# Six query products on GpSimd, b folded into ScalarE's scales in two groups, and a new order of all steps

## The chip, the core and the metric

The kernel runs on one core of a Trainium2 chip. The core has five engines with a queue each: TensorE (PE in the profile, its weight loads PEld), VectorE (DVE), ScalarE (ACT), GpSimd (POOL) and SyncE (SP), which here only issues DMA transfers. Within its queue an engine works strictly in order; between engines semaphores order the work. The metric is the device time of one execution in microseconds (us). Before the change it is 264.83 us, the median of three runs (264.46, 264.83 and 264.94).

## The reference: what is computed

An attention with sketched polynomial features, for 4 batches, 4 heads, 1088 positions and head size 32, whose output goes straight into a feed-forward layer with a rational activation:

```python
def phi(x):                                   # 8 x 8 = 64 features of one position
    a, b = S1 @ x, S2 @ x                     # 8 numbers each
    return outer(a, b)
kv = sum over positions of phi(k) v^T;  z = sum over positions of phi(k)
attn = (phi(q) kv) / (phi(q) z + 1e-6)
h = attn @ w_in                               # 4352 tokens x 2048
P = a0 + a1*h + a2*h**2 + a3*h**3
Q = 1.0 + abs(b0)*abs(h) + abs(b1)*h**2
out = (P / (Q + 1e-6)) @ w_out                # 4352 x 128
```

## The kernel before

**Queries.** The 1024 main positions of each of the four batches are taken in chunks of 512 (four blocks of 128). The very first chunk is cut into two halves, so there are nine chunks n = 0 to 8; a tenth, n = 9, holds the 64 remaining positions of all batches. Step names count them 0, 0b, 1, 2, ... 8, so chunk n = 3 is step number 2. For each chunk `add_queries` (L584) transposes q on PE, evacuates it on ACT, projects it to a, b and a denominator part on PE, and evacuates this as `abc` on ACT. From the second batch on two chunks make a pair: DVE computes the denominators of both, inverts them and scales a by them (`den_product` to `scale`, L627 to L641). Then `product` (L643) forms the 64 features per head as `q_p`, 128 partitions x 1024 float32, by one multiplication with broadcast operands. PE transposes `q_p` (`p_transposes`, "qp tr"), ACT evacuates it (`p_evac`, "qp ev"), PE multiplies it by kv ("x mm"), and ACT evacuates `xT` ("x ev"). There is one buffer of `q_p`, so a second product waits for the first one's transposes.

**Feed-forward.** `add_group` (L779) handles 23 groups of hidden columns, g = 0 to 22; most have 128 x 4096 values. PE computes h, ACT evacuates it as bfloat16 `hb` in pieces of 1024 ("hev"). The quotient is formed as P * exp(-ln Q), with Ln and Exp on ACT. `TERMS` (L158) picks one of four forms per group:

- "2" (groups 0 to 3 and 20 to 22) and "2d" (groups 6, 8, 10, 12, 15, 17, 19): DVE does absolute value, Q and P by multiplications; in "2d" the constant a1 is added by a DMA transfer that accumulates into y ("dadd1").
- "t" (groups 5, 7, 11, 13, 16, 18): DVE makes u = |h| with a bitwise operation ("abs", L820), the square `sq` ("sq", L914) and the square scaled by b1/b0 ("sqb", L919). A DMA transfer accumulates this onto u ("dq"), and Ln takes b0 as its scale.
- "s" (groups 4, 9, 14): ACT makes u = |b0 h| with one activation (`s_abs`, L807, "habs"), DVE scales the square by b1 (L919), the transfer accumulates, and Ln's scale is 1.

In "s" and "t" P comes from `sq` too: y = a3*sq + a1 ("n1"), sq becomes a2*sq + a0 ("n3"), y is multiplied by h ("n2"), and a second transfer adds `sq` to y ("dy"). In all forms y is finally multiplied by u ("n5") and goes to PE ("py").

**The order.** Every step is registered by `plan.add(engine, ns, function, after=..., take=..., give=...)`. The list `ORDER` (L19) names the 783 steps in the order in which they are issued; each engine's queue is that list restricted to its own steps. The durations in `plan.add` are bookings with which such a list can be planned; at run time they do nothing. The accumulating transfers are issued by POOL (`accumulate`, L895), in its queue's order. `HOT` (L162) gives numbers of matmuls on zeros that stand at places of PE's queue (L1071).

**The start.** SP loads the inputs in a fixed order; POOL prepares constants, copies v into place ("va 0", "va 1", L428) and copies the small weights (`s_weights`, L374).

Of the kernel before, what the change touches and what calls it, by code (L numbers as in the profile page):

```python
# [123 lines left out]
def kernel(  # L124
# [13 lines left out]
    nc = tc.nc  # L138
# [19 lines left out]
    TERMS = {**{g:"2d" for g in range(4,20)}, **{g:"s" for g in (4,9,14)}, **{g:"t" for g in (5,7,11,13,16,18)}}  # L158
# [3 lines left out]
    HOT = [2, 6, 23, 4, 18, 4, 3]  # L162
# [26 lines left out]
    def tile_of(pool, name, shape, dtype):  # L189
        return pool.tile(shape, dtype, name=name, bufs=BUFS[name])  # L190
# [124 lines left out]
    b_rel = consts.tile([128, 3], FP, name="b_rel")  # L315
# [74 lines left out]
    def rel_b():  # L390
        nc.vector.tensor_scalar(out=b_rel[:, 0:1], in0=b_abs[:, 0:1], scalar1=1e-18, scalar2=None, op0=AX.max)
        nc.vector.reciprocal(out=b_rel[:, 1:2], in_=b_rel[:, 0:1])
        nc.vector.tensor_mul(out=b_rel[:, 2:3], in0=b_rel[:, 1:2], in1=b_abs[:, 1:2])

    c_b = plan.add("DVE", 100, abs_b, after=[ld["ab"]], rank=-5)
    c_b = plan.add("DVE", 300, rel_b, after=[c_b], rank=-5) if "t" in USED else c_b
# [187 lines left out]
    def add_queries(n, nt, srcs, weights, kv_lhs, load_steps, kv_steps, w_steps, rank, give=(), early=False,  # L584
# [58 lines left out]
        def product():  # L643
            abc = T["abc", n][:, :G, :]
            T["q_p", n] = tile_of(att, "q_p", [128, JC * H, R * R], FP)
            nc.vector.tensor_mul(out=T["q_p", n][:, :G, :].rearrange("p g (i j) -> p g i j", i=R),
                                 in0=abc[:, :, 0:R, None].broadcast_to([128, G, R, R]),
                                 in1=abc[:, :, None, R:2 * R].broadcast_to([128, G, R, R]))
# [69 lines left out]
        def rest(s):  # L718
            s = plan.add("DVE", 68 + 1067 * G // 16, product, after=[s, T.get(("prod", n - 1)) if pair == 1 else None], rank=rank + 0.02, take=["q_p"],
# [59 lines left out]
    def add_group(g, G):  # L779
# [27 lines left out]
        def s_abs():  # L807
            T["u", g] = tile_of(moe, "u", [128, GW], BF)
            nc.scalar.activation(out=T["u", g][:, :gw], in_=T["hb", g][:, :gw], func=ACT.Abs, scale=b_abs[:, 0:1])  # L809
# [18 lines left out]
        def mul(out, in0, in1):  # L828
            return lambda: nc.vector.tensor_mul(out=out(), in0=in0(), in1=in1())  # L829

        def ln(l0, lw):
            T["L", g, l0] = tile_of(moe, "L", [128, LW], FP)
            nc.scalar.activation(out=T["L", g, l0][:, :lw], in_=T["u", g][:, l0:l0 + lw], func=ACT.Ln, bias=one_ap,  # L833
                                 scale=b_rel[:, 0:1] if terms == "t" else 1.0)
# [81 lines left out]
        def s_scaled():  # L916
            T["even", g] = tile_of(moe, "lin", [128, GW], BF)
            by = b_rel[:, 2:3] if terms == "t" else b_abs[:, 1:2]
            nc.vector.tensor_scalar(out=even(), in0=sq(), scalar1=by, scalar2=None, op0=AX.mult)  # L919

        def s_affine(out, c1, c0):
            def f():
                if out is y:
                    T["y", g] = tile_of(moe, "y", [128, GW], BF)
                nc.vector.tensor_scalar(out=out(), in0=sq(), scalar1=a_sb[:, c1:c1 + 1], scalar2=a_sb[:, c0:c0 + 1],  # L925
                                        op0=AX.mult, op1=AX.add)
            return f

        if square:
            sp = plan.add("DVE", tt, s_first, after=[he], rank=g - 0.5, take=["lin"], name=f"sq {g}")  # L930
            d2 = plan.add("DVE", ts + 61, s_scaled, after=[sp, c_b], rank=g - 0.5, take=["lin"], name=f"sqb {g}")
            d = add_tile("dq", u, even, [ha, d2], g - 0.5, give=["lin"])
# [17 lines left out]
        if square:  # L950
            p = plan.add("DVE", ts + 121, s_affine(y, 3, 1), after=[sp, ld["ab"]], rank=g - 0.3, take=["y"], name=f"n1 {g}")
            t = plan.add("DVE", ts + 121, s_affine(sq, 2, 0), after=[sp, d2, p, ld["ab"]], rank=g - 0.3, name=f"n3 {g}")
            p = plan.add("DVE", tt, mul(y, y, hb), after=[p, ha], rank=g - 0.3, give=["hb"], name=f"n2 {g}")
            p = add_tile("dy", y, sq, [p, t], g - 0.3, give=["lin"])
# [158 lines left out]
```

## Time and profile before

| | |
|---|---|
| median of three runs | 264.83 us |
| the profiled execution, its own time | 264.85 us |
| its span from first to last instruction | 263.1 us |
| DVE's query products of 1024 elements | 7, mean 1.22 us |
| ACT's absolute values (L809) | 3, mean 3.74 us |
| DVE's bitwise absolute values of 4096 | 12, mean 1.25 us |
| POOL's issues of accumulating transfers (L897) | 25, 1.17 to 1.98 us each |
| these transfers, issue to landing (median) | 8.4 us |

In the profile a row of a group reads: line, engine, operation, output <- inputs, shapes, count | busy us and mean ns of one | idle time of the engine before them and what ended it. A row in order of time reads: start, duration, engine, line, operation; idle time before it in brackets. Busy time of an engine counts instructions that wait inside themselves for a resource as busy. PE's ends are modelled, so a busy PE is not a PE at its peak.

### The profile page before, as it was taken

The page shows a single profiled execution, that of the slowest core. Times are in us where ns is not written, and L with a number is a line of the kernel's source. Part 1 is how long each engine was busy: PE and PEld are TensorE (multiplying, and loading weights), DVE is VectorE, ACT ScalarE, POOL GpSimd, SP SyncE. Part 2 cuts the span into 40 slices and gives each one's busy share as a digit, 9 for nine tenths or more (in the row PEclk, how much of TensorE's full clock was granted, in tenths as well). Part 3 has the DMA queues.
Part 4 walks back from the last instruction along what each step waited for, and adds up shares of the span by engine and source line. Part 5 has one row for each costly group of instructions (what it writes and reads, how often), then busy time and mean ns, then how long its engine had stood idle before and what let it go on. Part 6 is the DMA issues. An engine that isn't in the chain of part 4 may idle for free. (4 is left out here: it accounts for less than half of the span.)

```text
span 263.1 us, 3159 instructions
## 1 busy us (share of the span) xinstructions
PE 246.8 (94%) x1186; PEld 145.6 (55%) x1186; DVE 242.8 (92%) x240; ACT 238.6 (91%) x211; POOL 43.0 (16%) x63
## 2 busy tenths in 40 slices
PE   8999999999999999989899998999999899999971
PEld 4889898755656654434373645545434345554451
DVE  1658999979999999999999999999999999999992
ACT  3249798889989999999999999999999999999993
POOL 3700010101201113011201121101220202122000
PEclk9999999999999999999999999999999999999998
DMA  6969839952888996938798879972799896788812
GB/s 171 298 209 174 166 90 173 218 91 50 189 159 96 165 190 93 118 55 150 144 133 139 156 102 181 184 139 50 133 167 128 159 187 84 91 159 162 120 40 101
DMA packets 36607, 36.94 MB, mean 140 GB/s; under 512 B 18160, under 2 KB 30448, under 8 KB 36464
## 3 DMA queue, kind: packets, MB, share of 16 engines
q0 software_dynamic: 11664, 25.69, 62.6%
q1 hardware_dynamic: 24496, 10.95, 15.8%
q8 instruction: 9, 0.15, 0.2%
q10 hardware_dynamic: 432, 0.10, 0.2%
q14 instruction: 6, 0.05, 0.1%
HBM read 8.82 MB, written 2.23 MB: 42 GB/s over the span
## 5 line engine op out<-in xcount | busy, mean ns | idle before, releaser
L794 PE MATMUL h_ps<-xT,w_in_sb 128*128 128x512 f32 (+1 forms) x320 | 126.6, 533 | 0.9 <-ACT hb L800 0.9
L794 PEld LDWEIGHTS h_ps<-xT,w_in_sb 128*128 128x128 f32 x320 | 57.4, 190 | 43.4 <-issue 34.3
L800 ACT CAST hb<-h_ps 128x1024 bf16<-128x1024 f32 (+1 forms) x70 | 70.9, 1038 | 5.6 <-PE h_ps L794 5.4
L837 ACT ACTIVATE u<-L 128x4096 bf16<-128x4096 f32 (+3 forms) x23 | 63.7, 2768 | 0.3
L829 DVE TENSOR_TENSOR y<-y,hb 128x4096 bf16<-128x4096 bf16 (+3 forms) x37 | 58.7, 1595 | 0.1
L833 ACT ACTIVATE L<-u,one_ap 128x4096 f32<-128x4096 bf16 (+3 forms) x17 | 43.4, 2555 | 0.2 <-DVE u L829 0.2
L829 DVE TENSOR_TENSOR y<-y,u 128x4096 bf16<-128x4096 bf16 (+3 forms) x23 | 39.8, 1731 | 0.5 <-ACT u L837 0.3
L857 PEld LDWEIGHTS <-w_out 128*128 128x128 bf16 x208 | 20.2, 98 | 27.6 <-issue 11.8
L857 PE MATMUL out_ps<-y,w_out 128*128 128x512 bf16 (+1 forms) x144 | 30.8, 355 | 1.1 <-DVE y L829 1.1
L897 POOL DMA_DIRECT2D u<-lin x9 | 10.8, 1206 | 104.4 <-ACT ab L461 25.7
L833 ACT ACTIVATE L<-u,one_ap,b_rel 128x4096 f32<-128x4096 bf16 x6 | 23.2, 3875 | 0.0
L914 DVE TENSOR_TENSOR lin<-hb 128x4096 bf16<-128x4096 bf16 x9 | 20.6, 2287 | 0.0
L897 POOL DMA_DIRECT2D y<-lin x9 | 12.0, 1334 | 49.6 <-DVE y L829 15.7
L829 DVE TENSOR_TENSOR u<-lin,u 128x4096 bf16<-128x4096 bf16 (+3 forms) x14 | 19.2, 1375 | 0.2
L897 POOL DMA_DIRECT2D y<-zeros x7 | 12.3, 1760 | 41.6 <-PE h_ps L794 18.4
L820 DVE TENSOR_SCALAR u<-hb 128x4096 int16<-128x4096 int16 (+3 forms) x20 | 18.4, 918 | 0.5 <-ACT hb L800 0.3
L489 PEld LDWEIGHTS kv_ps<-v_aug,k_p 128*128 128x128 f32 x128 | 15.3, 192 | 1.1 <-issue 0.2
L489 PE MATMUL kv_ps<-v_aug,k_p 128*128 128x66 f32 x128 | 15.8, 272 | 0.0
L857 PE MATMUL out_ps<-u,w_out 128*128 128x512 bf16 (+1 forms) x64 | 13.7, 352 | 1.3 <-ACT u L837 1.1
L1075 PE MATMUL kv_ps<-const-float32-0.0 128*128 128x512 bf16 x60 | 14.2, 381 | 0.0
L661 ACT COPY q_pT<-w_ps 128x512 f32<-128x512 f32 (+1 forms) x20 | 10.5, 552 | 2.6 <-PE w_ps L654 2.6
L841 DVE TENSOR_SCALAR y<-hb,a_sb 128x4096 bf16<-128x4096 bf16 (+3 forms) x14 | 12.4, 886 | 0.0
(102 smaller groups left out, 274.1 us busy)
## 6 DMA issues: line engine op xcount, KB each, us to landing
u<-lin POOLq DMA_DIRECT2D x9, 1024.0 KB, 7.9
y<-lin POOLq DMA_DIRECT2D x9, 1024.0 KB, 8.2
y<-zeros POOLq DMA_DIRECT2D x6, 1024.0 KB, 11.0
out_dram<-oT SPq DMA_DIRECT2D x7, 256.0 KB, 2.7
kq<-in_k_dram SPq DMA_DIRECT2D x3, 512.0 KB, 5.0
v_aug<-in_v_dram SPq DMA_DIRECT2D x12, 128.0 KB, 4.7
kq<-in_q_dram SPq DMA_DIRECT2D x3, 512.0 KB, 4.8
w_in_sb<-in_moe_w_in_dram SPq DMA_DIRECT2D x1, 1024.0 KB, 6.9
```

The source lines that it names most:

```text
L489: nc.tensor.matmul(T["kv", b][:, hp * 66:(hp + 1) * 66], lhsT=lhs(hp), rhs=rhs(hp), start=(first and hp == 0), stop=final, skip_group_chec ...
L794: nc.tensor.matmul(T["h", g, s][:, i * W:(i + 1) * W], lhsT=w_in_sb[:, fi * 128:(fi + 1) * 128], rhs=T["xT", n][:, :W], start=True, stop=True)
L800: nc.scalar.copy(out=T["hb", g][:, s * W:(s + nsub) * W], in_=T["h", g, s][:, :nsub * W])
L820: nc.vector.tensor_scalar(out=u().bitcast(mybir.dt.int16), in0=hb().bitcast(mybir.dt.int16), scalar1=0x7FFF, scalar2=None, op0=AX.bitwise_and)
L829: return lambda: nc.vector.tensor_mul(out=out(), in0=in0(), in1=in1())
L833: nc.scalar.activation(out=T["L", g, l0][:, :lw], in_=T["u", g][:, l0:l0 + lw], func=ACT.Ln, bias=one_ap, scale=b_rel[:, 0:1] if terms == ...
L837: nc.scalar.activation(out=T["u", g][:, l0:l0 + lw], in_=T["L", g, l0][:, :lw], func=ACT.Exp, scale=-1.0)
L841: nc.vector.tensor_scalar(out=y(), in0=hb(), scalar1=a_sb[:, 3:4], scalar2=a_sb[:, 2:3], op0=AX.mult, op1=AX.add)
L857: nc.tensor.matmul(T["o", n][:, :W], lhsT=W_terms[w][:, fis[i], :], rhs=T[src, g][:, i * W:(i + 1) * W], start=(start and i == 0), stop=(s ...
L897: nc.gpsimd.dma_start(out=dst(), in_=src(), accum_op=AX.add, max_dma_last_dim=4096)
L914: nc.vector.tensor_mul(out=sq(), in0=hb(), in1=hb())
L1075: nc.tensor.matmul(hot_ps[0], lhsT=zero.broadcast_to([128, 128]), rhs=zero.broadcast_to([128, CW]), start=True, stop=True)
```

## The change

Six query products, those of chunks n = 3 to 8 (steps 2 to 7), are made by GpSimd instead of VectorE. Group 9 goes from form "s" to form "t". In the two groups left in form "s" (4 and 14), ScalarE now makes u = |h b0/b1|, the square is accumulated without being scaled, and Ln takes b1 as its scale; P's even part goes to a second tile, since the transfer now reads `sq` itself. `ORDER` and `HOT` are new.

```diff
-    TERMS = {**{g:"2d" for g in range(4,20)}, **{g:"s" for g in (4,9,14)}, **{g:"t" for g in (5,7,11,13,16,18)}}
+    TERMS = {**{g:"2d" for g in range(4,20)}, **{g:"s" for g in (4,14)}, **{g:"t" for g in (5,7,9,11,13,16,18)}}
...
-    HOT = [2, 6, 23, 4, 18, 4, 3]
+    QPOOL = {3,4,5,6,7,8}
+    HOT = [2, 2, 5, 11, 6, 14, 14, 4, 3]
...
-        nc.vector.tensor_scalar(out=b_rel[:, 0:1], in0=b_abs[:, 0:1], scalar1=1e-18, scalar2=None, op0=AX.max)
-        nc.vector.reciprocal(out=b_rel[:, 1:2], in_=b_rel[:, 0:1])
-        nc.vector.tensor_mul(out=b_rel[:, 2:3], in0=b_rel[:, 1:2], in1=b_abs[:, 1:2])
+        nc.vector.tensor_scalar(out=b_rel[:, 0:2], in0=b_abs[:, 0:2], scalar1=1e-18, scalar2=None, op0=AX.max)
+        nc.vector.reciprocal(out=b_rel[:, 2:4], in_=b_rel[:, 0:2])
+        nc.vector.tensor_mul(out=b_rel[:, 4:5], in0=b_rel[:, 2:3], in1=b_abs[:, 1:2])
+        nc.vector.tensor_mul(out=b_rel[:, 5:6], in0=b_rel[:, 3:4], in1=b_abs[:, 0:1])
...
-            nc.vector.tensor_mul(out=T["q_p", n][:, :G, :].rearrange("p g (i j) -> p g i j", i=R),
+            eng = nc.gpsimd if n in QPOOL else nc.vector
+            eng.tensor_mul(out=T["q_p", n][:, :G, :].rearrange("p g (i j) -> p g i j", i=R),
...
-            s = plan.add("DVE", 68 + 1067 * G // 16, product, after=[s, T.get(("prod", n - 1)) if pair == 1 else None], rank=rank + 0.02, take=["q_p"],
+            s = plan.add("POOL" if n in QPOOL else "DVE", 2300 * G // 16 if n in QPOOL else 68 + 1067 * G // 16, product, after=[s, T.get(("prod", n - 1)) if pair == 1 else None], rank=rank + 0.02, take=["q_p"],
...
-            nc.scalar.activation(out=T["u", g][:, :gw], in_=T["hb", g][:, :gw], func=ACT.Abs, scale=b_abs[:, 0:1])
+            nc.scalar.activation(out=T["u", g][:, :gw], in_=T["hb", g][:, :gw], func=ACT.Abs, scale=b_rel[:, 5:6])
...
-                                 scale=b_rel[:, 0:1] if terms == "t" else 1.0)
+                                 scale={"t": b_rel[:, 0:1], "s": b_rel[:, 1:2]}.get(terms, 1.0))
...
-            d2 = plan.add("DVE", ts + 61, s_scaled, after=[sp, c_b], rank=g - 0.5, take=["lin"], name=f"sqb {g}")
-            d = add_tile("dq", u, even, [ha, d2], g - 0.5, give=["lin"])
+            if wide_abs:
+                d1 = plan.add("DVE", ts + 121, s_affine(y, 3, 1), after=[sp, ld["ab"]], rank=g - 0.45, take=["y"], name=f"n1 {g}")
+                t = plan.add("DVE", ts + 121, s_affine(even, 2, 0), after=[sp, d1, ld["ab"]], rank=g - 0.45, take=["lin"], name=f"n3 {g}")
+                d = add_tile("dq", u, sq, [ha, t], g - 0.5, give=["lin"])
+            else:
+                d2 = plan.add("DVE", ts + 61, s_scaled, after=[sp, c_b], rank=g - 0.5, take=["lin"], name=f"sqb {g}")
+                d = add_tile("dq", u, even, [ha, d2], g - 0.5, give=["lin"])
```

The new order on POOL, from the first accumulating transfer on (q prod is a query product, the others are issues of transfers):

```
before: dq 4, dy 4, dq 5, dy 5, dadd1 6, dq 7, dy 7, dadd1 8, dq 9, dy 9, dadd1 10, dq 11, dy 11, dadd1 12, dq 13, dy 13, dq 14, dy 14, dadd1 15, ...
after:  dq 4, dy 4, q prod 2, dq 5, q prod 3, dy 5, dadd1 6, dq 7, dy 7, dadd1 8, q prod 4, dq 9, q prod 5, dy 9, dadd1 10, dq 11, dy 11, dadd1 12,
        dq 13, dy 13, q prod 6, q prod 7, dq 14, dy 14, dadd1 15, ...
```

On DVE, ACT and PE the steps change places nearly everywhere after the first 15; within a group their order is mostly kept. At the start POOL makes the weight copies of the first batch between "va 0" and "va 1" instead of after both. On SP only the stores of chunks 1 and 2 change places.

More of the change, by code (lines that the diff above doesn't have):

```diff
@@ L314 @@
     b_abs = consts.tile([128, 2], FP, name="b_abs")
-    b_rel = consts.tile([128, 3], FP, name="b_rel")
+    b_rel = consts.tile([128, 6], FP, name="b_rel")
     c_add = {i: zeros if i == ADDED[0] else big.tile([128, CW], FP, name=f"c_add{i}") for i in ADDED}
@@ L390, in rel_b @@
     def rel_b():
-        nc.vector.tensor_scalar(out=b_rel[:, 0:1], in0=b_abs[:, 0:1], scalar1=1e-18, scalar2=None, op0=AX.max)
-        nc.vector.reciprocal(out=b_rel[:, 1:2], in_=b_rel[:, 0:1])
-        nc.vector.tensor_mul(out=b_rel[:, 2:3], in0=b_rel[:, 1:2], in1=b_abs[:, 1:2])
+        nc.vector.tensor_scalar(out=b_rel[:, 0:2], in0=b_abs[:, 0:2], scalar1=1e-18, scalar2=None, op0=AX.max)
+        nc.vector.reciprocal(out=b_rel[:, 2:4], in_=b_rel[:, 0:2])
+        nc.vector.tensor_mul(out=b_rel[:, 4:5], in0=b_rel[:, 2:3], in1=b_abs[:, 1:2])
+        nc.vector.tensor_mul(out=b_rel[:, 5:6], in0=b_rel[:, 3:4], in1=b_abs[:, 0:1])
     c_b = plan.add("DVE", 100, abs_b, after=[ld["ab"]], rank=-5)
-    c_b = plan.add("DVE", 300, rel_b, after=[c_b], rank=-5) if "t" in USED else c_b
+    c_b = plan.add("DVE", 400, rel_b, after=[c_b], rank=-5) if USED & {"s", "t"} else c_b
     def scaled(i, col, half):
@@ L645, in product @@
             T["q_p", n] = tile_of(att, "q_p", [128, JC * H, R * R], FP)
-            nc.vector.tensor_mul(out=T["q_p", n][:, :G, :].rearrange("p g (i j) -> p g i j", i=R),
-                                 in0=abc[:, :, 0:R, None].broadcast_to([128, G, R, R]),
-                                 in1=abc[:, :, None, R:2 * R].broadcast_to([128, G, R, R]))
+            eng = nc.gpsimd if n in QPOOL else nc.vector
+            eng.tensor_mul(out=T["q_p", n][:, :G, :].rearrange("p g (i j) -> p g i j", i=R),
+                           in0=abc[:, :, 0:R, None].broadcast_to([128, G, R, R]),
+                           in1=abc[:, :, None, R:2 * R].broadcast_to([128, G, R, R]))
         def p_transposes(hp):
@@ L917, in s_scaled @@
             T["even", g] = tile_of(moe, "lin", [128, GW], BF)
-            by = b_rel[:, 2:3] if terms == "t" else b_abs[:, 1:2]
-            nc.vector.tensor_scalar(out=even(), in0=sq(), scalar1=by, scalar2=None, op0=AX.mult)
+            nc.vector.tensor_scalar(out=even(), in0=sq(), scalar1=b_rel[:, 4:5], scalar2=None, op0=AX.mult)
         def s_affine(out, c1, c0):
             def f():
-                if out is y:
-                    T["y", g] = tile_of(moe, "y", [128, GW], BF)
+                if out is not sq:
+                    name = "y" if out is y else "lin"
+                    T["y" if out is y else "even", g] = tile_of(moe, name, [128, GW], BF)
                 nc.vector.tensor_scalar(out=out(), in0=sq(), scalar1=a_sb[:, c1:c1 + 1], scalar2=a_sb[:, c0:c0 + 1],
@@ L950, in add_group @@
         if square:
[L951 to L954, printed above, removed]
+            if not wide_abs:
+                d1 = plan.add("DVE", ts + 121, s_affine(y, 3, 1), after=[sp, ld["ab"]], rank=g - 0.3, take=["y"], name=f"n1 {g}")
+                t = plan.add("DVE", ts + 121, s_affine(sq, 2, 0), after=[sp, d2, d1, ld["ab"]], rank=g - 0.3, name=f"n3 {g}")
+            p = plan.add("DVE", tt, mul(y, y, hb), after=[d1, ha], rank=g - 0.3, give=["hb"], name=f"n2 {g}")
+            p = add_tile("dy", y, even if wide_abs else sq, [p, t], g - 0.3, give=["lin"])
         else:
```

70 rows, old and new, of the table ORDER are left out of this document.

## The prediction

> **What bounds the kernel now.** I read the page's busy shares first, then busy time by stretch, then the groups of VectorE, ScalarE and GpSimd by shape, and last the order of time around the few places where GpSimd and VectorE work at once.
>
> ```profile
> PE 246.8 (94%) x1186; PEld 145.6 (55%) x1186; DVE 242.8 (92%) x240; ACT 238.6 (91%) x211; POOL 43.0 (16%) x63
> ```
>
> Three engines stand above 90%, so the average names no bound. Busy time by stretch does (columns: PE, PEld, DVE, ACT, POOL busy us with instruction counts, clock, DMA share, GB/s):
>
> ```profile
> 0.00:22.00 22.00, 20.14 (x130) 16.27 (x131) 9.69 (x24) 9.15 (x21) 7.83 (x38) 1.00 0.80 220
> 22.00:57.00 35.00, 35.00 (x210) 28.17 (x209) 33.25 (x59) 29.93 (x37) 2.51 (x2) 1.00 0.83 160
> 57.00:250.00 193.00, 185.62 (x777) 96.81 (x776) 191.84 (x143) 191.12 (x143) 32.66 (x23) 1.00 0.82 132
> 250.00:263.20 13.20, 6.09 (x73) 4.34 (x71) 8.00 (x18) 8.40 (x13) 0.00 (x0) 0.92 0.19 70
> ```
>
> From 57 to 250 us DVE is busy 191.8 of 193.0 us and ACT 191.1: both are full at once. DVE is also nearly full from 22 to 57 us (33.3 of 35.0), ACT is not (29.9). So every microsecond that DVE gains or loses after 22 us moves the end, a gain only until ACT's own work becomes the longer. PE has 14.2 us of matmuls on zeros in its busy time and is no bound. POOL has room in its queue; the question is whether its work lies beside DVE's.
>
> The prices, from the groups by shape (columns: busy us, mean ns of one, idle before):
>
> ```profile
> L646 DVE TENSOR_TENSOR q_p<-abc 128x1024 f32<-128x1024 f32 x7 | 8.5, 1221 | 0.1
> L919 DVE TENSOR_SCALAR lin<-lin,b_abs 128x4096 bf16<-128x4096 bf16 x3 | 3.9, 1285 | 0.1
> L820 DVE TENSOR_SCALAR u<-hb 128x4096 int16<-128x4096 int16 x12 | 15.0, 1247 | 0.1
> L809 ACT ACTIVATE u<-hb,b_abs 128x4096 bf16<-128x4096 bf16 x3 | 11.2, 3736 | 0.0
> L833 ACT ACTIVATE L<-u,one_ap 128x4096 f32<-128x4096 bf16 x9 | 34.1, 3793 | 0.0
> L833 ACT ACTIVATE L<-u,one_ap,b_rel 128x4096 f32<-128x4096 bf16 x6 | 23.2, 3875 | 0.0
> ```
>
> And the two engines side by side, in order of time (start, us, engine, instruction):
>
> ```profile
> 6.49 0.62 POOL L428 COPY v_aug<-q_p 128x512 f32<-128x512 f32 x1 [1.41 <-DMA q_p<-in_v_dram]
> ...
> 7.44 1.22 DVE L472 TENSOR_TENSOR k_p<-ab 128x1024 f32<-128x1024 f32 x1 [1.48 <-ACT ab L461]
> ...
> 8.25 0.89 POOL L428 COPY v_aug<-q_p 128x512 f32<-128x512 f32 x1 [1.14 <-DMA q_p<-in_v_dram]
> ...
> 8.58 1.63 DVE L472 TENSOR_TENSOR k_p<-ab 128x1024 f32<-128x1024 f32 x1
> ...
> 9.08 1.22 POOL L376 COPY W_abc<-S 128x64 f32<-128x64 f32 x1
> ...
> 11.81 0.77 POOL L376 COPY W_abc<-S 128x64 f32<-128x64 f32 x4
> ```
>
> POOL's first copy ran alone: 0.62 us. Its second fell into DVE's first key product, took 0.89 us and ended at 9.14. DVE's second product, the same instruction as the first, took 1.63 instead of 1.22 us: it ends 0.41 us late. The next POOL copy took 1.22 us, beside four later ones that need 0.77 together (0.23 each, 0.18 from start to start), and it ends 0.09 us after that DVE product. So here the two do not overlap: each waits for the other's instruction to end.
>
> **The change part by part.** DVE instructions overlap their neighbours by some 80 ns, so I count DVE from start to start:
>
> ```profile
> 171.41 1.23 DVE L646 TENSOR_TENSOR q_p<-abc 128x1024 f32<-128x1024 f32 x1
> 172.56 0.22 DVE L629 TENSOR_TENSOR den<-abc 128x64 f32<-128x64 f32 x1
> ...
> 178.97 1.28 DVE L919 TENSOR_SCALAR lin<-lin,b_abs 128x4096 bf16<-128x4096 bf16 x1
> 180.17 1.34 DVE L925 TENSOR_SCALAR y<-lin,a_sb 128x4096 bf16<-128x4096 bf16 x1
> ```
>
> 1. Six query products leave DVE: 6 x 1.15 = -6.9 us.
> 2. Groups 4 and 14 lose their scaled square (L919 with b_abs): 2 x 1.20 = -2.4 us on DVE. Their Ln takes its scale from memory: 3.88 for 3.79 us, group 9's too, 3 x 0.08 = +0.25 us on ACT.
> 3. Group 9 goes over to the bitwise absolute value: ACT loses 3.74 us, DVE gains 1.25 - 0.08 = +1.2 us. ACT in all: -3.5 us.
> 4. One more small product in the preparation of b, two operations a column wider: the rows of that line are 0.15 to 0.16 us, +0.2 us on DVE.
> 5. Six query products on POOL. The trace has no product there. From POOL's copies (0.23 us at 64 elements, 0.62 at 512: 0.86 ns per element and 0.18 us to begin) a pass over 1024 elements takes 1.06 us. The lower bound is one pass, 1.06 us. A far upper bound is 16 copies of 64 elements at 0.18 us, 2.9 us, since a product is 16 blocks of 8x8. I take two passes, 2.13 us, because the product reads two operands and the copies read one; the 512-element copy is the nearest row. What that does to DVE: the 0.62 us copy held DVE for 0.41 us, that is its duration less 0.21. So 1.92 us per product, 6 x 1.92 = +11.5 us (bounds 6 x 0.85 = 5.1 and 6 x 2.64 = 15.8). If nothing held DVE up it would be 0. DVE has no idle time after 57 us in which the products could hide, and nearly all that it does there reads two SBUF tensors or runs a wide tensor-scalar. That the latter waits too has a smaller witness: at 189.07 a bitwise absolute value took 1.45 us, where a POOL issue was running, against a mean of 1.25.
> 6. POOL's queue. Products 2 and 3, 4 and 5, 6 and 7 now stand ahead of the accumulating transfers of groups 5, 9 and 14. A product may wait for one DVE instruction (2.29 us for the longest) and then run 2.13: a transfer behind it is issued up to 4.4 us later. For the y transfer of group 9, behind product 5, DVE has between its source (n2 9) and its use (n5 9) eleven steps, some 18 us by their rows, against 1.2 us of issue and 8.2 of landing: cover for about 9 us. I cost it at 0. The same lag delays the product's transposes on PE and their evacuations on ACT, which now has 3.5 us less to do and a DVE to wait for: 0.
> 7. At the start, GpSimd's copies of the first weights move ahead of its second copy of v. They will be caught between the key products and v arrives up to 1 us later, at about 11 to 12 us, where its first matmul ran at 11.7 before; but the 0.41 us that this copy cost DVE goes. I take 0, bounds -0.4 and +0.5.
> 8. The new order elsewhere: DVE's idle time after 22 us is a few microseconds at most (1.2 us of it at 54 us). Bounds -1.5 and +1.5, taken 0, as no row prices it. The issues on SP keep their order but for two stores that change places, and one matmul on zeros more is 0.24 us on PE, beside other work.
>
> DVE's sum: -6.9 - 2.4 + 1.2 + 0.2 + 11.5 = **+3.6 us**. ACT's -3.5 us buys nothing once DVE is the longer. The profiled execution took 264.85 us (span 263.1), the median is 264.83, so the sum needs no correction: 264.85 + 3.6 = 268.4 us.
>
> One row shows DVE held, and its instruction was float32. [...]
>
> **The rivals.**
> - *The product is short or holds DVE for part of it only* (faster). [...] At one pass DVE's sum is -7.9 + 5.1 = -2.8: 262.0 us. With no stall at all DVE would fall by 7.9 us, but ACT, full from 57 us, by 3.5 only: 261.4 us, and about 260 if the new order also closes some of ACT's 5 us of idle time between 22 and 57 us. For it speaks that only one DVE instruction in this trace was held by a POOL copy, and that was a float32 one; against it that four POOL copies there were held by DVE in turn.
> - *POOL's lag stalls the chain as well* (slower still). Each product starts up to 2.29 us late; if three pairs push an accumulating transfer or ACT's next evacuation past its cover, each by 1 us, it gives 268.4 + 3 = 271.4 us. For it: one q_p buffer makes the second product of a pair wait for the transposes of the first. Against: the covers of step 6.
> - *The two sums cancel*: a stall near 1.3 us, within 0.2% of before, 264.8 us.
>
> **How the numbers follow.** Forecast (DVE held for about the whole product) 0.58, lag on top 0.12, short or partial hold 0.26, cancelling 0.04. The forecast's own range is 266.5 to 270 us. The range of 8 in 10 reaches down to the short hold's 262.0 and to 261.4 with some of the order's gain, 260.8, and up to 271, which takes in most of the lag's case. Differences below 0.2% (0.5 us) cannot be told from none here. Faster 0.26, same 0.04, slower 0.70.
>
> **What would show it.** In the changed profile: POOL rows of line 649, six, at 2.1 us and more (up to 4.4 with the wait before them); DVE's TENSOR_TENSOR and TENSOR_SCALAR of 4096 with single instructions 1.5 to 2.2 us above their 2.29 and 1.3, once per product; DVE busy near 246 us; ACT busy near 235 with idle time between 57 and 250 us of several microseconds, released by DVE. If DVE's durations stay at their means beside the products, step 5 is wrong and the time falls to about 261. If DVE stays full and shorter than before by 2 to 3 us, the product's size is wrong. If DVE itself idles after 57 us waiting for a transfer, step 6 is wrong.

## The result, and the profile after

The changed kernel takes **276.64 us** (median of 4 runs, 273.98 to 277.02) against 264.83: a ratio of **1.0429**, 95% interval 1.0399 to 1.0460. The forecast was 268.4 with a range of 260.8 to 271.0, and slower at 0.70. The direction was right; the size was missed by 8.2 us, and the time lies 5.6 us above the range. The profiled execution took 277.02 us, its span is 275.3. All ratios compare fast executions; one of the four of experiment 8 (276.58 us, over 1.5% above that kernel's fastest) counts as slow and is left out.

The busy shares of the changed kernel, and the six products among the costliest groups:

```profile
PE 250.4 (91%) x1175; PEld 148.3 (54%) x1187; DVE 244.5 (89%) x234; ACT 236.9 (86%) x210; POOL 61.8 (22%) x69
...
L649 POOL TENSOR_TENSOR q_p<-abc 128x1024 f32<-128x1024 f32 x6 | 19.4, 3231 | 22.3 <-ACT hb L803 13.0
```

DVE's busy time grew by only 1.7 us (242.8 before), ACT's fell by 1.7 (238.6). The span grew by 12.2. So 10.5 of the 12.2 us are DVE not working: span less busy time is 20.3 us before and 30.8 after; for ACT it is 24.5 and 38.4. The forecast had put its whole loss into busy time.

Busy time by stretch of the changed kernel (columns: PE, PEld, DVE, ACT, POOL busy us with instruction counts, clock, DMA share, GB/s):

```profile
0.00:22.00 22.00, 19.96 (x129) 16.33 (x131) 9.14 (x28) 9.41 (x20) 8.39 (x38) 1.00 0.83 225
22.00:57.00 35.00, 35.00 (x212) 28.13 (x211) 31.08 (x55) 29.80 (x38) 2.51 (x2) 1.00 0.82 157
57.00:250.00 193.00, 179.09 (x719) 93.82 (x728) 184.28 (x123) 178.20 (x137) 49.55 (x28) 0.97 0.77 124
250.00:275.40 25.40, 16.32 (x121) 9.97 (x120) 19.99 (x32) 19.46 (x18) 1.31 (x1) 0.93 0.52 105
```

Most of the loss is in the third row. DVE was busy 191.8 of these 193.0 us before and is busy 184.3 now; ACT went from 191.1 to 178.2, and the granted clock from 1.00 to 0.97. In the second row DVE is 2.2 us less busy than before (31.1 for 33.3). That comes with the new order and need not cost anything: experiment 9, which is no slower than before, has the same 31.1 there.

**DVE is held, as step 5 said.** VectorE and GpSimd of the changed kernel side by side, around the first pair of products (start, us, engine, instruction):

```profile
57.40 2.29 DVE L917 TENSOR_TENSOR lin<-hb 128x4096 bf16<-128x4096 bf16 x1
...
57.45 4.05 POOL L649 TENSOR_TENSOR q_p<-abc 128x1024 f32<-128x1024 f32 x1 [13.00 <-ACT hb L803]
...
59.61 2.98 DVE L823 TENSOR_SCALAR u<-hb 128x4096 int16<-128x4096 int16 x1
62.51 1.28 DVE L921 TENSOR_SCALAR lin<-lin,b_rel 128x4096 bf16<-128x4096 bf16 x1
...
65.11 2.69 POOL L649 TENSOR_TENSOR q_p<-abc 128x1024 f32<-128x1024 f32 x1
65.91 2.98 DVE L928 TENSOR_SCALAR y<-lin,a_sb 128x4096 bf16<-128x4096 bf16 x1
68.92 1.35 DVE L928 TENSOR_SCALAR lin<-lin,a_sb 128x4096 bf16<-128x4096 bf16 x1
```

The product is issued at 57.45, but a DVE instruction runs until 59.69; the product ends at 61.50, 1.81 us after that. The next DVE instruction, a bitwise absolute value that otherwise takes 1.22 us here, takes 2.98: 1.76 us too long. This excess over the usual time of the same instruction is called a hold below. DVE's y = a3*sq + a1 at 65.91 takes 2.98 where its twin behind it takes 1.35. The six holds are 1.76, 1.63, 1.70, 1.63, 1.38 and 1.05, together **9.2 us**; the forecast had 11.5. The fifth is shorter because two small instructions with one input (a sum at 180.09 and a reciprocal at 180.35, 0.23 and 0.21 us) ran beside the product unheld, the sixth because DVE was waiting for ACT for 0.62 us at its beginning.

**And something else waits.** The rows of the changed kernel's waits that grew most (engine, line, waited for: us in total, times, longest):

```profile
DVE W_abc L568 <- PE w_ps L559: 3.6, 2, 1.9
DVE y L844 <- PE out_ps L860: 3.3, 1, 3.3
```

```profile
ACT hb L803 <- PE h_ps L797: 11.2, 12, 3.1
ACT q_pT L664 <- PE w_ps L657: 5.1, 3, 2.3
```

The same rows of ACT before:

```profile
ACT hb L800 <- PE h_ps L794: 5.4, 10, 1.2
ACT q_pT L661 <- PE w_ps L654: 2.6, 2, 2.4
```

Neither of DVE's two rows was there before. PE, no bound before, now ends waits of both engines; why it does shows in order of time:

```profile
75.93 1.03 PE L860 MATMUL out_ps<-y,w_out 128*128 128x256 bf16 x8 [2.80 <-DVE y L832]
...
161.83 1.25 PE L860 MATMUL out_ps<-y,w_out 128*128 128x512 bf16 x4 [2.37 <-DVE y L832]
...
182.04 1.12 PE L657 MATMUL w_ps<-ident,q_p 128*128 128x128 f32 x8 [2.04 <-POOL q_p L649]
```

and in the clock of these stretches (columns as above):

```profile
73.60:77.00 3.40, 1.07 (x9) 0.98 (x9) 3.40 (x4) 3.40 (x1) 0.37 (x1) 1.00 0.79 143
77.00:80.40 3.40, 3.40 (x7) 1.46 (x6) 3.37 (x3) 0.33 (x2) 0.00 (x0) 0.52 0.92 165
...
162.40:165.80 3.40, 3.40 (x14) 2.02 (x11) 3.40 (x2) 3.40 (x4) 0.00 (x0) 0.51 1.15 132
182.90:186.30 3.40, 3.19 (x11) 1.01 (x8) 2.78 (x2) 1.83 (x3) 2.61 (x1) 0.51 0.22 40
```

Three times PE has to wait 2.0 to 2.8 us for DVE or for a product, and each time the clock is then halved for one stretch of 3.4 us. From 77.0 to 80.4 PE is busy throughout, while ACT does 0.33 us of work. Before, the clock was never lowered ahead of the kernel's end (1.00 from 0 to 258 us of 263.1). The halved stretches begin at 77.16, 162.50 and 182.97 us and last 3.412, 3.413 and 3.413 us: the second begins 85.33 us behind the first, 25 times the length of one, the third 20.48 us behind the second, 6 times.

What follows on DVE is late as well. Two of its waits behind the first two halved stretches:

```profile
83.60 2.29 DVE L917 TENSOR_TENSOR lin<-hb 128x4096 bf16<-128x4096 bf16 x1 [0.69 <-ACT hb L803]
171.96 0.29 DVE L568 TENSOR_TENSOR W_abc<-w_ps,mask 128x128 f32<-128x128 f32 x1 [1.89 <-PE w_ps L559]
```

### The profile page after: what moved, and what is told of

Same layout as the page of the kernel before. It is cut to its first block, busy times and chain, and to the rows that moved or that the text cites. A ratio compares the mean times of both kernels' runs of the same rounds, so it can differ in the third digit from the quotient of the medians.

```text
span 275.3 us, 3162 instructions
## 1 busy us (share of the span) xinstructions
PE 250.4 (91%) x1175; PEld 148.3 (54%) x1187; DVE 244.5 (89%) x234; ACT 236.9 (86%) x210; POOL 61.8 (22%) x69
## 4 chain that ended last, share of the span: by engine, by line
DVE 43%; PE 40%; ACT 8%; issue 6%; POOL 1%; DVEq 0%; ACTq 0%
DVE y L832 17%; PE h_ps L797 16%; PE out_ps L860 6%; PE kv_ps L491 5%; DVE u L823 5%; DVE lin L917 4%; ACT L L836 3%; DVE lin L828 3%; DVE y L844 3%; DVE y L928 2%; DVE lin L921 2%; DVE u L832 2%; ACT hb L803 2%; DVE lin L928 2%; PE w_ps L609 2%
## 5 line engine op out<-in xcount | busy, mean ns | idle before, releaser
L803 ACT CAST hb<-h_ps 128x1024 bf16<-128x1024 f32 (+1 forms) x70 | 69.1, 1001 | 11.4 <-PE h_ps L797 11.2
L832 DVE TENSOR_TENSOR y<-y,hb 128x4096 bf16<-128x4096 bf16 (+3 forms) x37 | 60.0, 1630 | 0.1
L836 ACT ACTIVATE L<-u,one_ap,b_rel 128x4096 f32<-128x4096 bf16 x9 | 34.4, 3820 | 0.0
L836 ACT ACTIVATE L<-u,one_ap 128x4096 f32<-128x4096 bf16 (+3 forms) x14 | 31.7, 2263 | 0.8 <-DVE u L832 0.8
L900 POOL DMA_DIRECT2D u<-lin x9 | 11.3, 1261 | 81.9 <-ACT u L812 31.4
L649 POOL TENSOR_TENSOR q_p<-abc 128x1024 f32<-128x1024 f32 x6 | 19.4, 3231 | 22.3 <-ACT hb L803 13.0
L917 DVE TENSOR_TENSOR lin<-hb 128x4096 bf16<-128x4096 bf16 x9 | 21.6, 2404 | 1.8 <-ACT hb L803 1.7
L823 DVE TENSOR_SCALAR u<-hb 128x4096 int16<-128x4096 int16 (+3 forms) x21 | 21.0, 1000 | 2.5 <-ACT hb L803 1.7
L900 POOL DMA_DIRECT2D y<-zeros x7 | 12.4, 1772 | 44.7 <-DVE y L832 26.2
L900 POOL DMA_DIRECT2D y<-lin x9 | 10.8, 1199 | 40.7 <-DVE y L832 8.5
L844 DVE TENSOR_SCALAR y<-hb,a_sb 128x4096 bf16<-128x4096 bf16 (+3 forms) x14 | 12.4, 883 | 3.3 <-PE out_ps L860 3.3
L928 DVE TENSOR_SCALAR y<-lin,a_sb 128x4096 bf16<-128x4096 bf16 x9 | 13.7, 1523 | 0.7 <-PE out_ps L860 0.5
```

Source lines behind the costliest of these rows:

```text
L803: nc.scalar.copy(out=T["hb", g][:, s * W:(s + nsub) * W], in_=T["h", g, s][:, :nsub * W])
L823: nc.vector.tensor_scalar(out=u().bitcast(mybir.dt.int16), in0=hb().bitcast(mybir.dt.int16), scalar1=0x7FFF, scalar2=None, op0=AX.bitwise_and)
L844: nc.vector.tensor_scalar(out=y(), in0=hb(), scalar1=a_sb[:, 3:4], scalar2=a_sb[:, 2:3], op0=AX.mult, op1=AX.add)
L900: nc.gpsimd.dma_start(out=dst(), in_=src(), accum_op=AX.add, max_dma_last_dim=4096)
L917: nc.vector.tensor_mul(out=sq(), in0=hb(), in1=hb())
```

## The experiments

The theory: the products hold DVE, and behind each held DVE the chain through PE is late as well (PE waits, halved clock). A first rival: the new order itself is the loss, wherever the products run. A second: POOL's queue (a product ahead of a transfer, a late product ahead of PE) is the loss, and the hold by itself is covered. Of each edit the lines that matter are shown. The times in this section are medians; "before" was run beside each group and lay between 264.56 and 264.88.

### 1. New order, products on VectorE

```diff
-    QPOOL = {3,4,5,6,7,8}
+    QPOOL = set()
```

> The changed kernel with all query products back on VectorE; the new order, group 9's new form and the folded scales stay. If GpSimd's products cause the whole loss (VectorE held by 9.1 us in the changed profile, and the waits behind it), VectorE's work is that of before less 2.4 plus 1.4 us and the time is 261 to 265 us. If the new order is itself the cause, VectorE idles without GpSimd too and the time stays above 268 us.

Measured: 270.88 us, 1.0239 (1.0222 to 1.0256). Without any product on GpSimd, the new order is still 6 us slower than before, though DVE's busy time is 241.9 us and below before's. Its middle stretch:

```profile
57.00:250.00 193.00, 180.79 (x740) 95.37 (x750) 187.63 (x134) 183.91 (x137) 32.87 (x23) 0.99 0.79 128
```

Neither DVE (187.6) nor ACT (183.9) is full; the longest rows of their waits behind the start name PE (DVE 3.6 us for `w_ps`, ACT 7.3 us for `h_ps`). Read by itself this speaks for the order as the loss; what it means is only seen with experiment 9.

### 2. Old order, products on GpSimd

```diff
-            nc.vector.tensor_mul(out=T["q_p", n][:, :G, :].rearrange("p g (i j) -> p g i j", i=R),
+            eng = nc.gpsimd if 3 <= n <= 8 else nc.vector
+            eng.tensor_mul(out=T["q_p", n][:, :G, :].rearrange("p g (i j) -> p g i j", i=R),
```

> The kernel before, with the same six query products moved to GpSimd and nothing else changed. If holding VectorE is all that the move does, 264.8 - 6.9 + 9.1 = 267.0 us. If the late products also stall TensorE and ScalarE whatever the order, 270 us and more. If the new order is the cause of the loss, 265 to 267 us.

Measured: 272.20 us, 1.0286 (1.0271 to 1.0301). The six holds sum to 8.8 us; DVE's busy time rises by 1.7 us (242.8 to 244.5: the products leave, the holds come), yet the time rises by 7.6. Here DVE itself stands still for a transfer, `lin` of group 14 waiting for the landing of the y transfer of group 13, which POOL issued behind a product:

```profile
DVE lin L920 <- DMA y<-lin: 3.1, 1, 3.1
```

The hold and the queue place both cost; experiments 10 and 13 separate them. From experiment 10, the same kernel with short products, to this one DVE's busy time grows by 7.8 us and the time by 4.8.

### 3. Before, with six spare products added on GpSimd

Six products that nobody reads are put on POOL behind six of the "dq" transfers; the rest of the kernel is untouched.

```diff
+                if name == "dq" and g in (9, 11, 13, 14, 16, 18):
+                    x = ident.rearrange("p (g i) -> p g i", i=R)
+                    spare = v_aug[0].rearrange("p h j d -> p (h j d)")[:, 0:1024].rearrange("p (g i j) -> p g i j", i=R, j=R)
+                    nc.gpsimd.tensor_mul(out=spare, in0=x[:, :, :, None].broadcast_to([128, 16, R, R]),
+                                         in1=x[:, :, None, :].broadcast_to([128, 16, R, R]))
```

> The kernel before, with six spare products of the same size on GpSimd behind the first accumulating issue of groups 9, 11, 13, 14, 16 and 18, which nobody waits for (they write memory that is no longer used); VectorE's own work is unchanged. If each holds VectorE as in the changed profile (1.05 to 1.73 us each), 264.8 + 6 x 1.5 = 274 us, with single VectorE instructions 1.0 to 1.7 us long of their kind. If GpSimd's products run beside VectorE, 264.8 us.

Measured: 276.99 us, 1.0467 (1.0451 to 1.0483). Nothing waits for these products, and still they cost 12.4 us. DVE's busy time rises by 11.4 (the holds sum to 11.3; three of them, of 2.43, 2.38 and 2.10 us, are longer than any in the changed kernel, and why is not shown). Its page, its middle stretch, and one of the holds with its product:

```profile
PE 247.8 (90%) x1174; PEld 145.9 (53%) x1186; DVE 254.2 (92%) x240; ACT 239.1 (87%) x211; POOL 65.5 (24%) x69
```

```profile
57.00:250.00 193.00, 176.09 (x718) 92.10 (x727) 192.22 (x128) 180.19 (x138) 53.15 (x28) 0.99 0.76 123
```

```profile
142.04 5.99 POOL L901 TENSOR_TENSOR v_aug<-ident 128x1024 f32<-128x1024 f32 x1
...
146.20 2.91 DVE L930 TENSOR_SCALAR lin<-lin,a_sb 128x4096 bf16<-128x4096 bf16 x1
```

DVE is full (192.2 of 193) and ACT, with the same work as before, is not (180.2). This product had to wait through two DVE instructions (5.99 us in all) and then held the next for about 1.6 us. The hold is a cost by itself, at 12.4 / 11.4 = 1.1 us per us. Since DVE waits for transfers only 0.8 us behind the start, this rules out that only POOL's queue is at fault.

### 4. Changed kernel, PE kept busy with matmuls on zeros

```diff
-    HOT = [2, 2, 5, 11, 6, 14, 14, 4, 3]
+    HOT = [2, 11, 5, 11, 6, 14, 14, 4, 3]
+    KEEP = {("u", 3): 22, ("u", 12): 10}
...
+            for _ in range(KEEP.get((src, g), 0)):
+                nc.tensor.matmul(T["o", n][:, :W], lhsT=zero.broadcast_to([128, 128]), rhs=zero.broadcast_to([128, W]),
+                                 start=False, stop=False, skip_group_check=True)
```

> The changed kernel with matmuls on zeros at the three places where TensorE waited over 2 us and the clock was halved for 3.4 us afterwards (22 of 256 columns behind the first projection of group 3, 10 of 512 behind that of group 12, 9 more in the second set of such matmuls before the transposes of query product 6). If the halved clock is what makes the waits dear, the granted clock stays at 1.00 up to the end and the time falls by 3 to 6 us, to 271 to 274 us. If it is not, 276 to 277 us.

Measured: 274.87 us, 1.0390 (1.0365 to 1.0415). In the profiled execution (274.31 us) the clock stays at 1.00 up to 250 us. The time falls by 1.8 us by the medians and by 1.0 us by the ratios, less than expected, and is uncertain by about 1.0 us. The middle stretch:

```profile
57.00:250.00 193.00, 182.53 (x765) 96.41 (x775) 186.49 (x125) 180.97 (x137) 49.59 (x28) 1.00 0.78 126
```

DVE and ACT are still far from full, so the halved clock is a consequence with a price of its own and not the cause of the rest. The waits of DVE at 83.60 and 171.96 shown above shrink to 0 and to 0.22 us, but its wait for a y buffer grows from 3.3 to 4.2. One of the chosen places, behind group 12, was not where the PE wait lies; there a wait of 2.37 us remained, and this time the clock was not lowered after it.

### 5. Old order, the changed forms, products on VectorE

ORDER and HOT of before, GpSimd without products, and

```diff
-                d = add_tile("dq", u, sq, [ha, t], g - 0.5, give=["lin"])
+                d = add_tile("dq", u, sq, [ha, sp], g - 0.5, give=["lin"])
```

so that the steps can stand where they stood before.

> The order and the zero matmuls of the kernel before, all query products on VectorE, but the changed forms: group 9 with the bitwise absolute value, groups 4 and 14 without the scaled square (its steps taken out of the order, the new absolute value put behind group 9's square). If the forms are a small gain, as the sum has it (VectorE -1.0 us, ScalarE -3.5), 262.5 to 264.3 us, and the 6.3 us that the new order cost with VectorE's products are the order's alone. If the forms themselves cost time, 265.5 us and more.

Measured: 265.25 us, 1.0024 (1.0013 to 1.0035). DVE has 1.5 us less work than before, ACT 3.0 us less, and the kernel is not faster. Middle stretch:

```profile
57.00:250.00 193.00, 184.43 (x776) 96.65 (x775) 190.77 (x141) 187.23 (x141) 32.08 (x23) 1.00 0.82 132
```

ACT's saving turned into idle time (187.2 for 191.1), DVE's too. In the old order, steps 2 and 3 of the forecast bought nothing.

### 6. Experiment 1, with two projections earlier

In ORDER of experiment 1, "zproj 1", the projection on PE of z (the sum of phi(k)) of batch 1, goes ahead of "h 5,0" (h matmuls of group 5), and "zproj 3" between "h 14,2" and "h 14,0", because DVE waited there for PE (1.7 and 1.9 us). In words:

```diff
+ 159 (zproj 1) ahead of h 5,0
+ 252 (zproj 3) between h 14,2 and h 14,0
- both at their later places
```

> The new order with all query products on VectorE, and in it two small steps of TensorE moved forward: the projection of z of batch 1 ahead of the first four h matmuls of group 5, that of batch 3 between the two sets of h matmuls of group 14 behind which it stood. VectorE stood 1.7 and 1.9 us at the steps that read them. If such places are what the new order costs, 267.0 to 268.0 us against 270.9; if VectorE only waits elsewhere then, 270 to 271 us.

Measured: 270.41 us, 1.0232 (1.0189 to 1.0276), not told apart from experiment 1. The two waits shrank to 0.2 and 0; in their place:

```profile
DVE den L632 <- ACT abc L621: 3.8, 3, 1.7
```

This row was 1.2 us in experiment 1. The steps behind the projections now waited for ACT's evacuations, 1.65 us where there had been no wait and 1.19 where there had been 0.20. A PE wait that DVE shows is not always PE's fault: removing it exposed the next one.

### 7. Experiment 1, with matmuls on zeros

```diff
+    KEEP = {("u", 3): 12, ("u", 10): 10}
```

and the loop of experiment 4.

> The new order with all query products on VectorE, with matmuls on zeros behind the first projections of group 3 (12 of 256 columns) and group 10 (10 of 512), where TensorE waited 1.5 and 2.4 us. There the clock was halved once, for 3.4 us. If the halved clock is a large part of what the new order costs, 267 to 269 us; if a small part, 269 to 270.5 us; if none, 270.9 us.

Measured: 269.55 us, 1.0178 (1.0161 to 1.0195); the clock stays at 1.00 up to 250 us. One halved stretch, behind a PE wait of 2.36 us, is worth 1.3 us in this kernel (1.6 by the ratios).

### 8. Only the first two pairs on GpSimd

```diff
-    QPOOL = {3,4,5,6,7,8}
+    QPOOL = {3,4,5,6}
```

> The changed kernel with query products 2 to 5 on GpSimd and 6 and 7 back on VectorE. If each product on GpSimd costs the same (5.8 us for six, between the new order with and without them), 274.7 us. If the last pair costs most, since TensorE waited 2.0 us for it, its clock was then halved and VectorE waited 3.3 us for a y buffer behind it, 271.5 to 273 us.

Measured: 272.98 us, the median of three executions from 271.67 to 275.02 (1.0321, 1.0263 to 1.0380). The question was whether the last pair is dearer than the first two; the interval covers both answers. It stays open.

### 9. Changed kernel, products cut to a sixteenth

```diff
+            M = 1 if n in QPOOL else G
-            eng.tensor_mul(out=T["q_p", n][:, :G, :].rearrange("p g (i j) -> p g i j", i=R),
+            eng.tensor_mul(out=T["q_p", n][:, :M, :].rearrange("p g (i j) -> p g i j", i=R),
```

(The two inputs are cut in the same way. The other fifteen sixteenths of these features are not computed; every later step keeps its size.)

> The changed kernel with the six products cut to a sixteenth on GpSimd (64 of 1024 elements; the rest of the features is left as the buffer has it, so this part of the computation is left out). VectorE is held up by next to nothing and is as short as the order was laid out for. If the new order is good as long as VectorE keeps to it, and the 6.3 us came from VectorE being 7 to 9 us longer than the order supposes, 257 to 261 us. If the order itself is the poorer one, 264 us and more.

Measured: **264.36 us**, 0.9988 (0.9974 to 1.0002). Everything of the change but the products' size, in the new order, with the new forms, POOL's queue and the new start, is worth -0.5 us and cannot be told from nothing. Its page and middle stretch:

```profile
PE 245.2 (93%) x1175; PEld 146.1 (56%) x1187; DVE 235.2 (90%) x234; ACT 236.2 (90%) x210; POOL 51.3 (20%) x69
```

```profile
57.00:250.00 193.00, 184.81 (x768) 97.52 (x778) 187.49 (x138) 189.48 (x142) 40.35 (x29) 1.00 0.82 132
```

From here to the changed kernel the only edit is the size of six products: +12.3 us. In spans (262.7 and 275.3) that is 9.3 us more DVE busy time and 3.3 us more DVE idle time. It also bears on experiment 1. This order is good while the products cost DVE next to nothing; put back on VectorE (6.7 us of busy time) they cost 6.5 us. So the order is not the loss where the products are short; where they stand on VectorE it is 6 us worse than the old one.

The other half is as telling: against before, DVE has 7.6 us less work and ACT 2.4 us less, for 0.5 us. From 57 to 250 us ACT stands at 189.5 of 193.

### 10. Old order, products on GpSimd cut to a sixteenth

Experiment 2 with the cut of experiment 9.

```diff
+            M = 1 if 3 <= n <= 8 else G
```

> The kernel before with the same six products cut to a sixteenth on GpSimd (the same part of the computation left out), its own order and forms. VectorE loses 6.9 us. If VectorE's time is what counts until ScalarE, full from 57 us, becomes the longer, 259.5 to 262.5 us; if an order once laid out gives nothing back when work is taken away, 264 to 265 us.

Measured: 267.43 us, 1.0109 (1.0084 to 1.0134): slower than before, although six products are off DVE and next to nothing holds it. GpSimd and VectorE of this kernel in order of time:

```profile
171.43 0.28 POOL L648 TENSOR_TENSOR q_p<-abc 128x64 f32<-128x64 f32 x1 [7.57 <-DVE den L629]
171.92 1.20 POOL L899 DMA_DIRECT2D y<-lin  x1 [0.21 <-issue]
...
181.52 1.29 DVE L921 TENSOR_SCALAR lin<-lin,b_abs 128x4096 bf16<-128x4096 bf16 x1 [2.94 <-DMA y<-lin]
```

and the same transfer in the kernel before:

```profile
168.04 1.20 POOL L897 DMA_DIRECT2D y<-lin  x1 [3.98 <-issue]
```

The transfer is issued 3.9 us later, behind a product that waits for the denominators; DVE then stands 2.94 us for its landing. Experiment 13 tests that the place in the queue is the cause.

### 11. Spare products of half the size

Experiment 3 with 512 elements instead of 1024.

```diff
-                    x = ident.rearrange("p (g i) -> p g i", i=R)
+                    x = ident[:, 0:64].rearrange("p (g i) -> p g i", i=R)
...
-                    nc.gpsimd.tensor_mul(out=spare, in0=x[:, :, :, None].broadcast_to([128, 16, R, R]),
+                    nc.gpsimd.tensor_mul(out=spare, in0=x[:, :, :, None].broadcast_to([128, 8, R, R]),
```

> The kernel before with six spare products of half the size (512 elements) at the places of the spare products before. If VectorE is held for as long as GpSimd reads, a half holds it 0.9 us and the loss halves, 264.8 + 6 = 271 us against 277.0. If each product costs the same whatever its size, 277 us.

Measured: 271.90 us, 1.0270 (1.0250 to 1.0290). Its page:

```profile
PE 249.4 (92%) x1174; PEld 147.5 (55%) x1186; DVE 249.4 (92%) x240; ACT 238.7 (88%) x211; POOL 60.1 (22%) x69
```

The holds sum to 6.2 us, DVE's busy time rises by 6.6, the time by 7.1: half the product, little over half of everything. The cost is not one per product but goes with its size.

### 12 and 14. Before, with b folded into the scales in groups 4, 9 and 14

The forms of the change without moving group 9 to the bitwise absolute value, in the old order; run twice, with 10 and 12 executions. Against the changed kernel:

```diff
-    TERMS = {**{g:"2d" for g in range(4,20)}, **{g:"s" for g in (4,14)}, **{g:"t" for g in (5,7,9,11,13,16,18)}}
+    TERMS = {**{g:"2d" for g in range(4,20)}, **{g:"s" for g in (4,9,14)}, **{g:"t" for g in (5,7,11,13,16,18)}}
```

> The kernel before with the folded scales alone, in all three groups of that form (4, 9 and 14): their scaled squares are gone, VectorE has 3 x 1.2 = 3.6 us less, less 0.2; ScalarE keeps its work. If VectorE's work sets the end, 261.4 to 262.5 us; if a stated order gives little of it back, as with the changed forms (265.25 us), 263.5 to 265 us.

> The kernel before with the folded scales in groups 4, 9 and 14, once more: 264.4 us against 264.8 if the small gain of the first time is real, 264.8 if it was scatter.

Measured: 264.44 us, 0.9986 (0.9976 to 0.9997), and the same kernel again 264.81 us, 1.0000 (0.9983 to 1.0016). DVE has 3.3 and 3.5 us less work. The first run looked like a small gain, the second does not show one; together there is none that can be told from nothing, and so no version here beats the kernel before.

### 13. Experiment 10, with the y transfer ahead of the product

```diff
- ... q prod 6, dy 13 ...   (POOL's order)
+ ... dy 13, q prod 6 ...
```

It leaves out the same part of the features as experiment 10.

> The old order with the six products cut to a sixteenth on GpSimd, as before, and one step moved: the issue of the second accumulating transfer of group 13 stands ahead of product 6 on GpSimd instead of behind it. If the place in GpSimd's queue caused the wait of 2.9 us, the time falls from 267.4 to about 264.5 us, and what then separates it from before is what 6.9 us less on VectorE are worth without a new order: nothing, if it stays at 264 to 265; if they are worth something, 261.4 to 263 us. If the wait had another cause, 267.4 us.

Measured: 264.64 us, 0.9994 (0.9975 to 1.0013). One transposition in POOL's queue is worth 267.43 - 264.64 = 2.8 us, the stall of 2.94. And with it gone, the time is that of before, with 6.0 us less DVE work:

```profile
57.00:250.00 193.00, 185.82 (x780) 97.12 (x779) 187.00 (x137) 191.40 (x143) 35.96 (x28) 1.00 0.82 132
```

ACT is full, 191.4 of 193.0, with the work it always had. This is the plainest witness of what taking work from DVE is worth in the old order.

## Why the prediction was wrong in size

Before and changed kernel, taken apart by experiment 9:

| | time, us | DVE busy, us | span less DVE busy, us |
|---|---|---|---|
| before | 264.83 | 242.8 | 20.3 |
| all of the change, products a sixteenth | 264.36 | 235.2 | 27.5 |
| the change | 276.64 | 244.5 | 30.8 |

- **Steps 1 to 3, the gains: this is the step that failed.** The sum credited -6.9, -2.4 and +1.2 us of DVE time to the end, with the order (step 8) at 0, under the sentence "every microsecond that DVE gains or loses after 22 us moves the end, a gain only until ACT's own work becomes the longer", and let the gains cancel against the holds. The busy times were about right (DVE -7.6 in the second row); their worth, order included, was 0.5 us. The first reading had itself shown ACT at 191.1 of 193.0 and had left ACT 3.5 us of room through step 3. In the old order experiment 13 (DVE -6.0, ACT as before: 0), 12 and 14 (DVE -3.3 and -3.5: 0) and 5 (DVE -1.5, ACT -3.0: +0.4) show that taking work from DVE buys nothing beside a full ACT, and that even the forms that relieve both gained nothing. In the new order the same products are worth 6.5 us when they leave VectorE (experiment 1 against 9), where ACT had room (183.9 of 193 us busy in experiment 1); but this order with the new forms costs 6.0 us first. So how the missing 7.4 us divide between the gains and the order depends on which is counted first. The rival with no hold, 261.4 us, had the same fault: experiment 9 comes close to it and stands at 264.36.
- **Step 4, b's preparation**, +0.2: not told apart by any run.
- **Step 5, the hold: right in kind, a fifth too large.** 9.2 us for 11.5, since the product is 1.81 us from the end of the DVE instruction before it, not 2.13, and the last pair held DVE for 1.38 and 1.05 only. The wide tensor-scalar instructions (1.76, 1.63, 1.70 and 1.63 us) and the bfloat16 multiplications of the last pair (1.38 and 1.05) are held as the one float32 product had been (0.41); that they would be was the author's estimate. The rival of a short or partial hold is out: the six holds average 1.5 us, above the 7.9 / 6 = 1.3 us (the gains over the six products) below which it begins.
- **Step 6, the lag, taken as 0: wrong by about 3 us.** Behind the 9.3 us of holds stand 3.3 us of DVE idle time that the short products do not have. The traces, compared instruction by instruction, show where. At 83.60, 87.12, 91.09, 110.13 and 171.96 us, all behind the first two halved stretches, DVE waits 3.0 us more than experiment 9 does; with the clock kept up (experiment 4) all of this is gone, and 0.9 comes back at the wait for a y buffer. At the sixth product DVE waits 0.2 us more, with the clock kept up too. So the halved clock carries most of this idle time; in the time of the kernel it is worth 1.0 to 1.8 us, give or take 1.0 (experiment 4). The wait for a y buffer at 199.5 (3.3 us, released by PE's projections) is no witness, since experiment 9 has one of 3.1 us as well; nor did this idle time take up any of the holds. The lag rival had 3 us for this, but on top of a sum that already held the gains.
- **Step 6, POOL's queue**: in the old order a product ahead of a transfer costs 2.8 us (experiments 10 and 13). In the new order no row of DVE's waits names a transfer behind the start: the cover counted there was enough.
- **Step 7, the start**: not told apart, but it is the same in experiment 9, which is no slower than before.
- **Step 8, the order, 0**: with short products nothing speaks against it (with the other parts, -0.5). It is no order for products on VectorE, though: experiment 1 is 6 us slower than before, and the bounds of 1.5 us did not reach that far.

So 264.85 - 0.5 (everything but the products' size) + 9.2 (holds) + 3.1 (the rest of the 12.3 us) gives the 276.6 measured; the 3.1 is a difference, not a measured part. The forecast's 268.4 has 7.4 us of gains and 2.3 us of hold too many, and leaves the 3.1 out. Two of these errors partly cancel: the hold taken too large hid 2.3 us of the miss.

Of the signs named ahead: rows of line 649 between 2.1 and 4.4 us came (2.6 to 4.0), single DVE instructions 1.5 to 2.2 us longer came for four of six (1.05 and 1.38 are below), DVE near 246 and ACT near 235 came as 244.5 and 236.9. ACT's idle time between 57 and 250 us came as well, but as 14.8 us and released mostly by PE, not by DVE. These were signs of the mechanism, and they fit a time far from 268.4: the one sign on DVE's idle time asked only for waits on a transfer, and DVE waited for PE and ACT.

What stays open: why experiment 9, with less work on DVE and on ACT, gains only 0.5 us. ACT's 2.4 us less work became 2.0 us more idle time, 1.6 of it between 57 and 250 us, where the longest single wait is 0.92 us at 193.41 for PE's transposes; whether such waits could be removed was not tried.

## What to carry to other kernels

Two engines were nearly full here and fed each other (DVE 191.8 and ACT 191.1 of 193.0 us), and a sum with signs on one engine's queue forecast too well: 268.4 us for 276.64. Work added to DVE moved the end here by 1.0 to 1.3 us per us (before to experiments 3 and 11, experiment 9 to 1 and to the changed kernel), and by 0.6 in one place (experiment 10 to 2, where DVE was busy 184.6 of 193 us; why less there is not shown). Work taken from DVE moved it by nothing where ACT was full (experiments 12, 13 and 14), and by about all of it where ACT had room (experiment 1 to 9). So price additions in full, price removals by the slack of the other engine in the order at hand, and never let them cancel. And an engine whose instructions hold the bound one up is no free place: what is moved there must be cheaper in held time (1.5 us per product here) than it was on the bound engine (1.15).

## What was not expected of the hardware

- The held time goes with the size of GpSimd's instruction: from the end of the DVE instruction before it, a product of 1024 float32 elements takes 1.81 us and one of 512 takes 0.90; DVE's own product of 1024 takes 1.22. Where nothing held GpSimd up, the two took 1.94 and 1.22 us (experiments 2 and 11).
- The clock was halved after PE waits of 2.04 to 2.80 us in the changed kernel and of 1.86 us in experiment 11, each time for one stretch of 3.4 us, with starts whole multiples of its length, 3.413 us, apart (25 and 6 in the changed kernel, 15 in experiment 11). The length of the wait alone does not decide: one of 2.37 us did it in the changed kernel, another of 2.37 us did not in experiment 4. What else decides is not shown. The clock goes with the spread of the changed kernel's runs, from 273.98 us (mean clock 0.988) to 277.02 (0.975); that it makes the spread was not tried separately.
